# Row scatters in pairs behind the Fourier steps, and the first rows of the second part turned during the last batch

## The chip, the cores and the metric

The kernel runs on one core of a Trainium2 chip. The metric is the device time of one execution in microseconds. The kernel before takes 3161.35 us, the median of 3 runs (3157.11 to 3165.08).

## The reference

The three stages of the reference are chained; each takes the rows of the one before it. In short:

```python
# x: (8, 3072, 256)
X = np.fft.fft(np.fft.fft(x, axis=1), axis=2).real       # 24576 rows of 256
# mixture of experts: 8 experts, 256 -> 1024 -> 256, the best one only
do_compute = X @ w_skip > 0                               # other rows pass unchanged
e_idx = argmax(X @ w_gate);  gate = softmax(...)[e_idx]
out[do_compute] = X + gate * (relu(X @ w1[e]) @ w2[e])    # e = e_idx of the row
# feed-forward layer with a rational activation, 256 -> 2048 -> 256
h = out @ w_in
P = a0 + a1*h + a2*h**2 + a3*h**3
Q = 1 + |b0|*|h| + |b1|*h**2
return (P / (Q + 1e-6)) @ w_out
```

## The kernel before

All matrix products run on TensorE (PE) in f16 with each f32 operand split into a high and a low f16 half, three products for one. The program has two parts that follow each other.

*The Fourier stage* goes through the 8 batches. A batch is 12 steps of the loop over `n` (12 x 8 + 2 passes in all, since the third transform runs `LA` = 2 steps behind). In a step, `s1` makes a part of the first transform of the *next* batch (two of three steps do, and ACT and DVE or PE bring it to the tiles o1h and o1l), `s2` makes the second transform of two groups of 128 rows, and `s3` the third transform of the step two back. `s2` ends with an ACT conversion of the PSUM tile u to the f16 tile o2h (L264) and a DVE subtraction for the low half o2l; both live in a pool of three buffers. `s3` reads them on PE and writes finished rows of 258 floats (256 values, the row's number and its gate) into row buffers, of which some lie in the space of the weights `mw`, others in the tile `third`.

POOL does two things in this stage. From the second batch on it makes the low half xl of the input for three of eight chunks (`by_pool`, L202; the others are made on DVE). And it scatters the finished rows to their place in the array XS in DRAM: experts' rows sorted by expert from its beginning, rows that skip the experts from `SKIP0`. The scatters are indirect DMAs, issued by POOL, 24 in a batch with 128 rows each (L361). Their addresses come from `route_steps`, a generator that is started when a batch is finished and is advanced once per step: seven pieces of softmax, comparison and prefix sums, then one pair of scatters per advance. So the scatters of batch b are written at steps 12b+20 to 12b+31; those of batch 6 begin at step 92, and what is left of them behind the last step (97) is written out at one go (`for r in late`). The eighth batch is scattered in the second part, three at a time, between its steps.

Each engine works through its instructions in the order in which the code issues them, and a wait blocks everything behind it on its engine. Nothing reorders, so the code's order is the order on each engine. DMAs that the SP or ACT engine issues stand in that engine's row too: a DMA that waits for its input blocks the ones behind it.

*The second part* takes tiles of 512 rows (of XS) through the feed-forward layer, eight steps a tile, 384 in all, and the expert layer beside it. Its first tile is rows that skip the experts: `load_skip(0)` loads them after the scatters of batches 0 to 5, `z_begin` calls `split_turned`, which casts the rows to f16 on ACT (L885), subtracts on DVE (L886) and turns high and low halves with one transposing DMA from SP (L888). The first matmul of the part, `u<-turned,wi` (L897), needs the turned rows and wi, the high and low halves of the layer's first weights, which SP loads at L675 just ahead of wo (L676). Those weights were decoded from the input's bytes by `decode_steps` during the Fourier stage, through the tiles wf, wm and ws.

Two variables keep row positions: `carry` counts the rows that each expert and the skip group have so far, and for the skip rows the first positions are kept free of later batches by a maximum, so that a tile of rows may be loaded while later scatters still run (the groups `scat` and `scat7` say which DMAs need no order among each other).

Of the kernel before, what the change touches and what calls it, by code (L numbers as in the profile page):

```python
# [8 lines left out]
F32 = mybir.dt.float32  # L9
F16 = mybir.dt.float16  # L10
I32 = mybir.dt.int32
AF = mybir.ActivationFunctionType
ALU = mybir.AluOpType
# [9 lines left out]
NG = 24  # L23
TILE = 512
# [105 lines left out]
def program(tc, x, w_skip, w_gate, w1, w2, w_in, w_out, a, b, f1, cs, tw, tok, ut, small, lt8, slot, out):  # L130
# [3 lines left out]
    with es:  # L134
# [16 lines left out]
        scat = []  # L151

        fa = ExitStack()
        xp = fa.enter_context(tc.tile_pool(name="xp", bufs=4))
# [3 lines left out]
        o2p = fa.enter_context(tc.tile_pool(name="o2p", bufs=3))  # L158
        low = fa.enter_context(tc.tile_pool(name="low", bufs=1))
        low.tile([128, 4 * ROW], F32, name="below")  # L160
        rwp = fa.enter_context(tc.tile_pool(name="rwp", bufs=1))
# [85 lines left out]

        o2 = {}

        def s2(bb, gp):  # L250
            u = ps.tile([128, 2, 512], F32, tag="u", name="u")
            for s in range(2):
                g = 2 * gp + s
                o = u[:, s, 0:CB]
                n = 0
                for h in range(2):
                    lh = o1[bb, "h"][:, h].rearrange("p c q -> p (c q)")[:, g * 128:g * 128 + 128]
                    ll = o1[bb, "l"][:, h].rearrange("p c q -> p (c q)")[:, g * 128:g * 128 + 128]
                    for st, mv in ((lh, 0), (lh, 1), (ll, 0)):
                        pe.matmul(o, lhsT=st, rhs=f2t[:, h, mv, :], start=(n == 0), stop=(n == 5))  # L260
                        n += 1
            th = o2p.tile([128, 2, CB], F16, tag="o2h", name="o2h")
            tl = o2p.tile([128, 2, CB], F16, tag="o2l", name="o2l")
            act.activation(th[:], u[:, :, 0:CB], AF.Copy, scale=2.0 ** -8)  # L264
            dve.scalar_tensor_tensor(out=tl[:], in0=u[:, :, 0:CB], scalar=2.0 ** -8, in1=th[:], op0=ALU.mult, op1=ALU.subtract)
            o2[bb, gp] = (th, tl)

        rows = {}
# [50 lines left out]
        def route_steps(bb, new_u, per=2):  # L319
# [30 lines left out]
            dve.tensor_tensor(out=rk, in0=u[:, 0, 0:216].rearrange("p (g c) -> p g c", c=9), in1=carry[:, None, :].to_broadcast([128, NG, 9]), op=ALU.add)  # L350
            dve.tensor_tensor(out=carry[:], in0=carry[:], in1=u[:, 0, 216:225], op=ALU.add)
            if bb == B - 3:
                dve.tensor_scalar(out=carry[:, 8:9], in0=carry[:, 8:9], scalar1=float(SKIP0 + R0 * TILE), scalar2=None, op0=ALU.max)
                dve.tensor_scalar(out=carry[:, 0:1], in0=carry[:, 0:1], scalar1=float(R1 * HALF), scalar2=None, op0=ALU.max)
# [4 lines left out]
            yield  # L359
            for g in range(NG):  # L360
                i = pool.indirect_dma_start(out=XS[:, :], out_offset=IndirectOffsetOnAxis(ap=si[:, g:g + 1], axis=0),  # L361
                                            in_=rws[g // 4][:, g % 4, :], in_offset=None, bounds_check=NROWS - 1, oob_is_err=False)
                if scat:
                    tc.declare_no_dep(i.ins, group="scat", reason="every slot is given once")
                tc.add_to_no_dep_group("scat", i.ins)
                if bb >= B - 2:
                    tc.add_to_no_dep_group("scat7", i.ins)
                scat.append(i.ins)
                if g % per == per - 1:
                    yield  # L370

        def decode_steps():
# [13 lines left out]
            for n in range(8):  # L386
# [5 lines left out]
                f = wp.tile([128, 1024], F32, tag="wf", name="wf")  # L392
                m = wp.tile([128, 1024], F32, tag="wm", name="wm")
                fi = f[:].bitcast(I32)
                dve.tensor_scalar(out=fi, in0=hw, scalar1=3, scalar2=0x3FFFFFFF, op0=ALU.logical_shift_left, op1=ALU.bitwise_and)
                dve.scalar_tensor_tensor(out=fi, in0=hw, scalar=-0x40000000, in1=fi, op0=ALU.bitwise_and, op1=ALU.bitwise_or)
                yield
                act.activation(m[:], hw.bitcast(F32), AF.Abs)
                dve.scalar_tensor_tensor(out=fi, in0=lw, scalar=29, in1=fi, op0=ALU.logical_shift_right, op1=ALU.bitwise_or)
                yield  # L400
                dve.scalar_tensor_tensor(out=f[:], in0=m[:], scalar=TINY, in1=f[:], op0=ALU.is_ge, op1=ALU.mult)
                yield
                sc = 16.0 if n < 4 else 256.0
                st = wp.tile([128, 2, 1024], F16, tag="ws", bufs=2, name="ws")
                act.activation(st[:, 0, :], f[:], AF.Copy, scale=sc)
# [195 lines left out]
        s1_lo()  # L601
        late = []
        prep = decode_steps()
        coeff = coefficients()
# [4 lines left out]
        for n in range(12 * B + LA):  # L609
            bb, gp = divmod(n, 12)  # L610
            s1_hi()
            if bb < B:
                s2(bb, gp)
            if n >= LA:
# [23 lines left out]
            if n >= 12:  # L638
                next(coeff, None)
                if n % 4 == 0:  # L640
                    next(coeff, None)
        for r in late:
            for _ in r:
                pass
# [11 lines left out]
        wk = pool_of("wk", 1)  # L656
        xtp = pool_of("xtp", 2)
        xsp = pool_of("xsp", 2)
# [163 lines left out]

        xt = {}

        def load_skip(s):
            t = xtp.tile([128, 4, ROW], F32, tag="xt", name="xt")
            if s < R0:
                i = sp.dma_start(out=t[:], in_=XS[SKIP0 + s * TILE:SKIP0 + (s + 1) * TILE, :].rearrange("(p r) c -> p r c", p=128))
                tc.declare_no_dep(i.ins, group="scat7", reason="the last batches write behind these rows")
                if s == 0:  # L830
                    after(i.ins, scat[:NG * (B - 2)])
                tc.add_to_no_dep_group("early", i.ins)
            else:
                r = reg(sp, C_SKIP + s, NROWS - TILE)
                i = sp.dma_start(out=t[:], in_=rows_of(r, TILE))
                after(i.ins, fills)
            xt["S", s] = t
# [43 lines left out]

        def split_turned(src, nr, tag):

            rows = rsp.tile([128, 2, nr, D], F16, tag=tag, name="rows")
            act.activation(rows[:, 0], src, AF.Copy)  # L885
            dve.tensor_tensor(out=rows[:, 1], in0=src, in1=rows[:, 0], op=ALU.subtract)  # L886
            t = xsp.tile([128, 2, nr, 2, 128], F16, tag=tag, name="turned")
            sp.dma_start_transpose(out=t[:].rearrange("p l r h c -> p (l r h) c"), in_=rows[:].rearrange("p l r d -> p (l r d)"))  # L888
            return t[:, 0], t[:, 1]
# [29 lines left out]
        def moe_begin(t):  # L919
            return split_turned(t[:, :, 0:D], 2, "m")  # L920

# [44 lines left out]
        def z_begin(src, ids, n):  # L966
            Z[n] = dict(x=split_turned(src[:, :, 0:D], 4, "z"), ids=ids)

# [97 lines left out]

        for s in range(2):
            load_skip(s)
        last = route_steps(B - 1, lambda: psm.tile([128, 2, D], F32, tag="m", name="acc"), 3)
# [188 lines left out]
```

## Time and profile before

| | |
|---|---|
| median of 3 runs | 3161.35 us |
| the profiled execution | 3152.81 us |
| its span in the trace | 3151.0 us |
| PE busy | 2944.4 us (93%) |
| DVE busy | 2816.8 us (89%) |
| ACT busy | 2536.1 us (80%) |
| POOL busy | 1391.3 us (44%) |

The span is the time from the first to the last instruction that the trace holds; the profiled execution took 1.8 us more. PE, DVE and ACT are the matrix, vector and activation engines, POOL is GpSimd, and SP issues DMAs. The busy shares are averages over two parts with different limits: in the Fourier stage, up to about 520 us, every engine has idle time, and in the second part PE has little. The granted clock is TensorE's, as a share of 2.4 GHz: 1.00 is that level, 0.50 is 1.2 GHz.

### The profile page before, as it was taken

Reading aid. Unit: us, or ns where it says so; the run is one execution under the profiler, and the core shown is the slowest. Engines: PE = TensorE matmul, PEld = TensorE weight load, DVE = VectorE, ACT = ScalarE, POOL = GpSimd, SP = SyncE. Lnnn points to the kernel's source line nnn. Section 1 sums busy time; section 2 is a strip of 40 time slices with the busy share of each in tenths; the row PEclk is TensorE's granted clock in tenths of the full one; section 3 lists DMA queues with packets and bytes.
Section 4 is the critical chain, followed back from the end, with each engine's and each line's share of the span. In section 5 each row is a group of like instructions: output and inputs, shape, how many; then the busy total and the mean of one; then the engine's idle time right before and its main releaser. Section 6 shows DMA issues by size and latency. Waiting matters only on the chain.

```text
span 3151.0 us, 56948 instructions
## 1 busy us (share of the span) xinstructions
PE 2944.4 (93%) x22994; PEld 2146.2 (68%) x22994; DVE 2816.8 (89%) x2969; ACT 2536.1 (80%) x2758; POOL 1391.3 (44%) x796
## 2 busy tenths in 40 slices
PE   8877864899999999999999999999999999999995
PEld 7666642577667777777777777777777777777764
DVE  6767644999999999999999999999999999999896
ACT  7666634698879889889889888888888888888884
POOL 0455534544334444444444444444444444444444
PEclk9989877999999999999999999999999999999998
DMA  8444443322312222213222311112112111211100
GB/s 237 148 145 133 157 161 114 92 84 68 108 41 68 55 88 85 67 45 93 82 58 65 86 43 34 40 57 67 35 41 81 45 31 41 84 38 28 31 18 14
DMA packets 230368, 236.85 MB, mean 75 GB/s; under 512 B 166995, under 2 KB 190932, under 8 KB 227156
## 3 DMA queue, kind: packets, MB, share of 16 engines
q1 hardware_dynamic: 209364, 174.23, 20.3%
q0 software_dynamic: 18432, 50.55, 4.6%
q10 hardware_dynamic: 2304, 8.39, 0.7%
q8 instruction: 181, 2.97, 0.4%
q14 instruction: 87, 0.71, 0.1%
HBM read 190.69 MB, written 77.05 MB: 85 GB/s over the span
## 4 chain that ended last, share of the span: by engine, by line
PE 75%; DVE 13%; issue 5%; ACT 3%; DMA 3%; another core or an unknown queue 1%; POOL 0%; SPq 0%; DVEq 0%; ACTq 0%; POOLq 0%
PE accz L907 26%; PE u L897 26%; PE acc L907 7%; PE e L897 7%; DVE gh L1000 4%; PE u L260 3%; DVE T L982 2%; DVE V L1005 2%; DMA out<-ob,ids 2%; PE u L245 1%; DVE gl L1012 1%; PE u L310 1%; DVE hl L915 1%; PE u L308 1%
## 5 line engine op out<-in xcount | busy, mean ns | idle before, releaser
L1006 POOL TENSOR_TENSOR V<-T,V 128x1024 f32<-128x1024 f32 x384 | 913.5, 2379 | 1369.8 <-DVE V L1005 1364.8
L897 PE MATMUL u<-turned,wi 128*128 128x512 f16 x4608 | 1065.3, 381 | 38.6 <-DMA turned<-rows 20.3
L907 PE MATMUL accz<-wo,gh 128*128 128x256 f16 x6144 | 1032.4, 273 | 5.9 <-ACT ob L1028 5.9
L907 PE MATMUL accz<-wo,gl 128*128 128x256 f16 x3072 | 839.9, 273 | 20.4 <-DVE gl L1012 18.0
L1000 DVE SCALAR_TENSOR_TENSOR gh<-T,co,Y 128x1024 f16<-128x1024 f32 x384 | 804.5, 2095 | 0.0
L897 PEld LDWEIGHTS <-wi 128*128 128x128 f16 x4608 | 452.7, 98 | 508.9 <-issue 50.7
L980 ACT ACTIVATE T<-u,co 128x1024 f32<-128x1024 f32 x384 | 462.8, 1205 | 331.3 <-PE u L897 202.5
L907 PEld LDWEIGHTS <-gh 128*128 128x128 f16 x6144 | 603.1, 98 | 159.3 <-issue 8.5
L982 DVE SCALAR_TENSOR_TENSOR T<-T,co,u 128x1024 f32<-128x1024 f32 x384 | 487.6, 1270 | 68.0 <-ACT Y L981 61.4
L1012 DVE SCALAR_TENSOR_TENSOR gl<-V,co,Y 128x1024 f16<-128x1024 f32 x384 | 489.0, 1274 | 28.8 <-POOL V L1006 28.8
L1005 DVE SCALAR_TENSOR_TENSOR V<-V,co,gh 128x1024 f32<-128x1024 f32 x384 | 490.3, 1277 | 0.0
L986 ACT ACTIVATE V<-Y,co 128x1024 f32<-128x1024 f32 x384 | 440.4, 1147 | 25.8 <-DVE gl L1012 25.6
L990 ACT ACTIVATE Y<-V,co 128x1024 f32<-128x1024 f32 x384 | 441.2, 1149 | 0.0
L981 ACT ACTIVATE Y<-u,co 128x1024 f32<-128x1024 f32 x384 | 426.3, 1110 | 0.0
L994 ACT ACTIVATE Y<-Y 128x1024 f32<-128x1024 f32 x384 | 404.3, 1053 | 0.0
L907 PEld LDWEIGHTS <-gl 128*128 128x128 f16 x3072 | 301.4, 98 | 60.1 <-DVE gl L1012 22.1
L897 PE MATMUL e<-turned,mw 128*128 128x256 f16 x2496 | 307.7, 273 | 8.1 <-DMA turned<-rows 8.1
L907 PE MATMUL acc<-mw,hh 128*128 128x256 f16 x1664 | 278.1, 273 | 0.0
L897 PEld LDWEIGHTS <-mw 128*128 128x128 f16 x2496 | 244.8, 98 | 37.3 <-issue 8.4
L1029 POOL DMA_INDIRECT out<-ob,ids x192 | 232.8, 1213 | 64.1 <-issue 46.4
L907 PE MATMUL acc<-mw,hl 128*128 128x256 f16 x832 | 226.8, 273 | 0.0
L361 POOL DMA_INDIRECT xs<-mw,rt x132 | 136.2, 1032 | 115.0 <-DVE rt L358 43.5
(201 smaller groups left out, 2942.5 us busy)
## 6 DMA issues: line engine op xcount, KB each, us to landing
mw<-wd SPq DMA_DIRECT2D x50, 2048.0 KB
xt<-in_x SPq DMA_DIRECT2D x64, 384.0 KB
xm<-xs SPq DMA_DIRECT2D x52, 258.0 KB
wf<-in_moe_w SPq DMA_DIRECT2D x48, 256.0 KB
wd<-ws SPq DMA_DIRECT2D x48, 256.0 KB
xt<-xs SPq DMA_DIRECT2D x22, 516.0 KB
wd<-ws ACTq DMA_DIRECT2D x16, 512.0 KB
wr<-in_moe_w_in SPq DMA_DIRECT2D x4, 1024.0 KB
```

Of the source, the lines that this page charges most:

```text
L897: pe.matmul(u[:, s, :], lhsT=sta, rhs=mv[:, :, k, :], start=(n == 0), stop=(n == 5))
L907: pe.matmul(acc[:, r, :], lhsT=sta[:, c], rhs=mv, start=(first and r % 2 == 0 and s == 0 and n == 0), stop=(last and s == nf - 1 and n == ...
L980: act.activation(d["T"], d["u"], AF.Square, scale=A[0], bias=A[1])
L981: act.activation(d["Y"], d["u"], AF.Abs, scale=A[4])
L982: dve.scalar_tensor_tensor(out=d["T"], in0=d["T"], scalar=A[2], in1=d["u"], op0=ALU.add, op1=ALU.mult)
L986: act.activation(d["V"], d["Y"], AF.Square, bias=A[5])
L990: act.activation(d["Y"], d["V"], AF.Ln, bias=A[6])
L994: act.activation(d["Y"], d["Y"], AF.Exp, scale=-1.0)
L1000: dve.scalar_tensor_tensor(out=h[:], in0=d["T"], scalar=A[a0], in1=d["Y"], op0=ALU.add, op1=ALU.mult)
L1005: dve.scalar_tensor_tensor(out=d["V"], in0=d["V"], scalar=A[c], in1=h[:], op0=ALU.add, op1=ALU.mult)
L1006: pool.tensor_tensor(out=d["V"], in0=d["T"], in1=d["V"], op=ALU.subtract)
L1012: dve.scalar_tensor_tensor(out=l[:], in0=d["V"], scalar=A[a0], in1=d["Y"], op0=ALU.add, op1=ALU.mult)
```

## The change

The change has two halves.

*Pairs behind the steps.* In the batches 0 to 6, a POOL copy of one column (`tick`) stands ahead of every pair of scatters. It reads the o2h that the step before made (`seen[0]`), so the pair can't go before that step's conversion on ACT is done. The copy is a reader of o2h, and ACT's conversion three steps later, which writes the same buffer, waits for it.

*The first 512 rows.* At step 86 SP loads the first skip rows (`row0`) behind the scatters of batches 0 to 3; at step 92 ACT casts them, at step 93 DVE subtracts and SP turns them (`turned0`). The second part begins with these instead of casting and turning its own. So that these rows are final by then, `carry` for the skip group gets a lower limit after batch 3, and the group `scat7` takes the scatters from batch 4 on.

To make room, wm now lies in the tile ws, a spacer pool `low` is gone, and the second part's tiles xt and turned alternate between two pools with one buffer each, of which one (`xta`, `xza`) is made before the Fourier stage.

```diff
+        xta = es.enter_context(tc.tile_pool(name="xta", bufs=1))
+        xza = es.enter_context(tc.tile_pool(name="xza", bufs=1))
...
-        low = fa.enter_context(tc.tile_pool(name="low", bufs=1))
-        low.tile([128, 4 * ROW], F32, name="below")
...
+        seen = [None]
+        tick = cst.tile([128, 1], F32, name="tick")
...
+            return th
...
+            if bb == 3:
+                dve.tensor_scalar(out=carry[:, 8:9], in0=carry[:, 8:9], scalar1=float(SKIP0 + TILE), scalar2=None, op0=ALU.max)
...
             for g in range(NG):
+                if g % per == 0 and bb < B - 1:
+
+                    pool.tensor_copy(out=tick[:].bitcast(F16)[:, 0:1], in_=seen[0][:, 0, 0:1])
                 i = pool.indirect_dma_start(out=XS[:, :], out_offset=IndirectOffsetOnAxis(ap=si[:, g:g + 1], axis=0),
                                             in_=rws[g // 4][:, g % 4, :], in_offset=None, bounds_check=NROWS - 1, oob_is_err=False)
                 if scat:
                     tc.declare_no_dep(i.ins, group="scat", reason="every slot is given once")
                 tc.add_to_no_dep_group("scat", i.ins)
-                if bb >= B - 2:
+                if bb >= 4:
...
-                m = wp.tile([128, 1024], F32, tag="wm", name="wm")
+                st = wp.tile([128, 2, 1024], F16, tag="ws", bufs=2, name="ws")
+                m = st[:].rearrange("p l n -> p (l n)").bitcast(F32)
...
-                act.activation(m[:], hw.bitcast(F32), AF.Abs)
+                act.activation(m, hw.bitcast(F32), AF.Abs)
...
             s1_hi()
+            seen[0] = this
             if bb < B:
-                s2(bb, gp)
+                this = s2(bb, gp)
...
+            if n == 86:
+                row0 = xta.tile([128, 4, ROW], F32, tag="xt", name="xt")
+                i = sp.dma_start(out=row0[:], in_=XS[SKIP0:SKIP0 + TILE, :].rearrange("(p r) c -> p r c", p=128))
+                tc.declare_no_dep(i.ins, group="scat7", reason="the later batches write behind these rows")
+                for sc in scat[:4 * NG]:
+                    tc.add_manual_dep(i.ins, sc.name, SYNC, reason="the rows")
+                tc.add_to_no_dep_group("early", i.ins)
+            if n == 92:
+                f = wp.tile([128, 1024], F32, tag="wf", name="wf")
+                half = f[:].bitcast(F16).rearrange("p (l r d) -> p l r d", l=2, r=4)
+                act.activation(half[:, 0], row0[:, :, 0:D], AF.Copy)
+            if n == 93:
+                dve.tensor_tensor(out=half[:, 1], in0=row0[:, :, 0:D], in1=half[:, 0], op=ALU.subtract)
+                turned0 = xza.tile([128, 2, 4, 2, 128], F16, tag="z", name="turned")
+                sp.dma_start_transpose(out=turned0[:].rearrange("p l r h c -> p (l r h) c"), in_=half.rearrange("p l r d -> p (l r d)"))
...
-        xtp = pool_of("xtp", 2)
+        xtp = pool_of("xtp", 1)
+        xzb = pool_of("xzb", 1)
...
-        xt = {}
+        xt = {("S", 0): row0}
 
         def load_skip(s):
-            t = xtp.tile([128, 4, ROW], F32, tag="xt", name="xt")
+            t = (xta, xtp)[s % 2].tile([128, 4, ROW], F32, tag="xt", name="xt")
...
-                if s == 0:
+                if s == 1:
...
-            Z[n] = dict(x=split_turned(src[:, :, 0:D], 4, "z"), ids=ids)
+            x = split_turned(src[:, :, 0:D], 4, "z", (xza, xzb)[n % 2]) if n else (turned0[:, 0], turned0[:, 1])
+            Z[n] = dict(x=x, ids=ids)
...
-        for s in range(2):
-            load_skip(s)
+        load_skip(1)
```

What moves on the engines is shown at three places. On POOL, at the start of the program, the first xl and then the scatters of batch 0 (in a row "x10" stands for ten of the same kind that follow each other). Before:

```order
L202 TENSOR_TENSOR xl<-xt,xh 96x1024 x4
L361 DMA xs<-mw,rt 132096x258 x10
L202 TENSOR_TENSOR xl<-xt,xh 96x1024
L361 DMA xs<-mw,rt 132096x258 x2
L202 TENSOR_TENSOR xl<-xt,xh 96x1024
L361 DMA xs<-mw,rt 132096x258 x4
```

On POOL at the same place after the change:

```order
L203 TENSOR_TENSOR xl<-xt,xh 96x1024 x4
L369 COPY tick<-o2h 128x1
L370 DMA xs<-mw,rt 132096x258 x2
L369 COPY tick<-o2h 128x1
L370 DMA xs<-mw,rt 132096x258 x2
L369 COPY tick<-o2h 128x1
```

The ten scatters that stood without anything between them are now five pairs, each behind a copy; the xl stand where they stood.

On ACT, the last steps of the last batch, with the semaphores that each instruction waits for (DVE, PE, Pool and Activation are engines, DMAHW queues of DMAs); ev is the third transform's way out of PSUM. Before:

```order
L264 ACTIVATE o2h<-u 128x552 [waits DVE_49,PE_49]
L314 ACTIVATE ev<-u 128x276 [waits DVE_49,PE_49,Activation_49]
L264 ACTIVATE o2h<-u 128x552 [waits DVE_49,PE_49]
L314 ACTIVATE ev<-u 128x276 [waits DVE_49,PE_49,Activation_49] x3
L433 DMA wd<-ws 128x2048
L885 ACTIVATE rows<-xt 128x1024 [waits DMAHW4_49,DMAHW2_49]
```

On ACT in the last batch after the change:

```order
L267 ACTIVATE o2h<-u 128x552 [waits DVE_49,PE_49,Pool_49]
L318 ACTIVATE ev<-u 128x276 [waits DVE_49,PE_49,Activation_49]
L664 ACTIVATE wf<-xt 128x1024 [waits DMAHW7_49]
L267 ACTIVATE o2h<-u 128x552 [waits DVE_49,PE_49,Pool_49]
L318 ACTIVATE ev<-u 128x276 [waits DVE_49,PE_49,Activation_49]
```

The conversion to o2h waits for POOL as well, and the cast of the first rows (L885 before) stands four conversions ahead of the last one (L664).

On SP, the queue that loads the weights and the rows, from the last raw weights (wr) to the beginning of the second part. Before:

```order
L420 DMA wr<-in_moe_w 128x4x256 x2
L675 DMA wi<-wd 128x8192
L676 DMA wo<-wd 128x8192
L828 DMA xt<-xs 128x1032 x2
L888 DMA_TRANSPOSE turned<-rows 128x16x128
L828 DMA xt<-xs 128x1032
```

On SP at the same place after the change:

```order
L429 DMA wr<-in_moe_w 128x4x256 x2
L656 DMA xt<-xs 128x1032
L668 DMA_TRANSPOSE turned<-wf 128x16x128
L703 DMA wi<-wd 128x8192
L704 DMA wo<-wd 128x8192
L856 DMA xt<-xs 128x1032 x2
```

The load of the first rows and their turning stood behind the loads of wi and wo and now stand ahead of them.

## Rows read from the trace of the kernel before

**Rows 1.** The page: span, busy times, and PE's busy tenths in 40 slices.

```profile
span 3151.0 us, 56948 instructions
...
PE 2944.4 (93%) x22994; PEld 2146.2 (68%) x22994; DVE 2816.8 (89%) x2969; ACT 2536.1 (80%) x2758; POOL 1391.3 (44%) x796
...
PE   8877864899999999999999999999999999999995
```

**Rows 2.** Windows: stretch, length, PE PEld DVE ACT POOL busy, clock, DMA share, GB/s.

```profile
31.58:72.03 40.45, 38.73 (x476) 32.06 (x474) 29.82 (x54) 33.68 (x50) 2.14 (x1) 0.99 0.75 232
72.03:124.02 51.99, 44.54 (x524) 35.45 (x522) 41.64 (x107) 37.40 (x56) 18.12 (x13) 0.94 0.52 158
124.02:185.01 60.99, 47.70 (x526) 37.40 (x525) 39.50 (x102) 37.16 (x55) 32.27 (x28) 0.91 0.46 141
...
302.35:368.51 66.16, 50.18 (x525) 38.93 (x523) 43.85 (x103) 37.83 (x56) 32.05 (x27) 0.87 0.45 138
368.51:448.46 79.95, 51.42 (x524) 38.72 (x522) 33.65 (x94) 36.40 (x54) 45.20 (x41) 0.79 0.43 141
448.46:516.42 67.96, 31.34 (x325) 25.73 (x323) 31.39 (x96) 16.09 (x31) 23.41 (x24) 0.75 0.43 153
...
124.02:448.46 324.44, 242.71 (x2609) 188.71 (x2608) 200.45 (x502) 187.22 (x279) 174.83 (x150) 0.87 0.46 142
```

**Rows 3.** POOL timeline: start, length, instruction, and idle time before it in brackets.

```profile
149.67 0.97 POOL L361 DMA_INDIRECT xs<-third,rt  x1 [0.31 <-issue]
150.63 0.13 POOL L574 MEMSET co<- 128x1 f32 x1
150.95 0.97 POOL L361 DMA_INDIRECT xs<-third,rt  x1 [0.19 <-issue]
```

**Rows 4.** Windows inside POOL's runs of scatters.

```profile
408.10:413.20 5.10, 5.10 (x65) 4.26 (x63) 4.80 (x8) 2.87 (x6) 4.12 (x4) 1.00 0.22 78
433.70:438.90 5.20, 0.87 (x3) 0.41 (x4) 0.00 (x0) 0.00 (x0) 3.90 (x4) 0.50 0.28 102
...
129.90:140.30 10.40, 9.44 (x123) 8.04 (x122) 7.97 (x23) 8.51 (x13) 8.18 (x7) 1.00 0.55 156
...
480.42:505.72 25.30, 4.50 (x35) 2.60 (x32) 2.04 (x5) 1.03 (x2) 19.51 (x20) 0.62 0.29 104
413.20:438.90 25.70, 6.87 (x42) 3.74 (x41) 1.24 (x3) 2.08 (x3) 19.53 (x21) 0.60 0.42 144
```

**Rows 5.** Windows of four steps, edges at o2h conversions, with L361 (row scatters) alone.

```profile
102.32:124.02 21.70, 10.89 (x10) 0.86 0.52 170
189.09:204.42 15.33, 7.28 (x7) 1.00 0.35 105
372.26:389.55 17.29, 8.63 (x8) 1.00 0.69 222
```

**Rows 6.** Lines of POOL, 72 to 448 us: busy, mean ns, idle before.

```profile
L202 POOL TENSOR_TENSOR xl<-xt,xh 96x1024 f16<-96x1024 f32 x18 | 41.6, 2309 | 97.4 <-issue 55.3 <-ACT xh L194 42.0
```

**Rows 7.** Timelines of ACT, DVE and PE where the second part begins.

```profile
509.86 1.06 ACT L885 ACTIVATE rows<-xt 128x1024 f16<-128x1024 f32 x1
...
511.28 1.22 DVE L886 TENSOR_TENSOR rows<-xt,rows 128x1024 f16<-128x1024 f32 x1
...
516.42 1.86 PE L897 MATMUL u<-turned,wi 128*128 128x512 f16 x4 [20.34 <-DMA turned<-rows]
```

**Rows 8.** SP timeline: the load of wi and the turn of the first rows.

```profile
445.27 0.45 SPq L675 DMA_DIRECT2D wi<-wd  x1
...
512.52 1.74 SPq L888 DMA_TRANSPOSE turned<-rows  x1
```

**Rows 9.** Window in which the loads of wi and wo ran.

```profile
446.00:464.00 18.00, 12.21 (x126) 10.13 (x125) 10.13 (x27) 7.68 (x15) 0.00 (x0) 0.96 0.88 350
```

More of the change, by code (lines that the diff above doesn't have):

```diff
@@ L397, in decode_steps @@
                 yield
-                act.activation(m[:], hw.bitcast(F32), AF.Abs)
+                act.activation(m, hw.bitcast(F32), AF.Abs)
                 dve.scalar_tensor_tensor(out=fi, in0=lw, scalar=29, in1=fi, op0=ALU.logical_shift_right, op1=ALU.bitwise_or)
                 yield
-                dve.scalar_tensor_tensor(out=f[:], in0=m[:], scalar=TINY, in1=f[:], op0=ALU.is_ge, op1=ALU.mult)
+                dve.scalar_tensor_tensor(out=f[:], in0=m, scalar=TINY, in1=f[:], op0=ALU.is_ge, op1=ALU.mult)
                 yield
                 sc = 16.0 if n < 4 else 256.0
-                st = wp.tile([128, 2, 1024], F16, tag="ws", bufs=2, name="ws")
                 act.activation(st[:, 0, :], f[:], AF.Copy, scale=sc)
@@ L602, in program @@
         late = []
+        this = None
         prep = decode_steps()
@@ L880, in fill, with split_turned @@
                     yield
-        def split_turned(src, nr, tag):
+        def split_turned(src, nr, tag, to):
             rows = rsp.tile([128, 2, nr, D], F16, tag=tag, name="rows")
@@ L886, in split_turned @@
             dve.tensor_tensor(out=rows[:, 1], in0=src, in1=rows[:, 0], op=ALU.subtract)
-            t = xsp.tile([128, 2, nr, 2, 128], F16, tag=tag, name="turned")
+            t = to.tile([128, 2, nr, 2, 128], F16, tag=tag, name="turned")
             sp.dma_start_transpose(out=t[:].rearrange("p l r h c -> p (l r h) c"), in_=rows[:].rearrange("p l r d -> p (l r d)"))
@@ L919, in moe_begin @@
         def moe_begin(t):
-            return split_turned(t[:, :, 0:D], 2, "m")
+            return split_turned(t[:, :, 0:D], 2, "m", xsp)
         def moe_steps(t, w, xh, xl, xf, ids, k):
```

## The prediction

> **What bounds the kernel now.** I read the page first, then the windows view cut at the o2h conversions (L264) that open the batches, then the POOL timeline, then short windows inside POOL's runs of scatters. The span is 3151.0 us; the second part, where TensorE is 9 tenths or more busy nearly throughout, takes from about 520 us to the end [rows 1, 2]. No term of mine comes from there. Everything that the change touches lies before 540 us.
>
> In the Fourier stage no engine is full. The first batch, which runs before any row is scattered, takes 40.45 us for its 12 steps. The next takes 51.99 us and the five behind it 324.44, that is 64.9 each (the first 60.99, the last 79.95), although PE's count of matmuls hardly grows (476, then 524 to 526) and DVE is busy for 39.5 to 43.9 us in a batch of 61 to 66 [rows 2]. What grew is POOL: 24 row scatters per batch (L361), one every 1.28 us when they follow each other [rows 3].
>
> The short windows show where the time goes. With four scatters in a run, PE was busy in all 5.10 us. Some 20 scatters into the same run it was busy for 0.87 of 5.20 us, with DVE and ACT at nothing and the clock granted at 0.50, the 1.2 GHz level. From the fifth scatter to the 24th PE was busy for 6.87 of 25.70 us in this run and for 4.50 of 25.30 in the next batch's, DVE for one or two [rows 4]. The DMA engines are only 0.28 to 0.42 busy there, so it is not their share that is short. Six scatters with two xl subtractions (L202) between them, 10.4 us, left PE 9.44 us busy [rows 4]. So a scatter alone holds nothing; a run of them, from about the fifth on, holds everything until it ends. What inside the chip does that no row here tells; I use it as an observation.
>
> **The change part by part.** *Pairs behind a step.* Each pair of scatters now stands behind a POOL copy that reads the previous step's o2h, so POOL can't run through ten or 24 scatters at a stretch while TensorE is at one step. In batches 1 to 6 this makes two scatters in each step. What a step then costs I take from two stretches of before that look so already: four steps from one o2h conversion to the fifth, 15.33 us with 7 scatters and 17.29 us with 8 [rows 5], together 4.08 us a step. Twelve are 48.9; I take 49.
> Batches 2 to 6 took 324.4 us [rows 2]; five of 49 are 245: 79.4 saved. In batch 1 the scatters begin with its ninth step, at 102.32 us [rows 5]; from there to 124.02 are 21.7 us for four steps, which become 16.3: 5.4 saved.
> Bounds: a step can't be shorter than DVE's work, 39.5 to 43.9 us a batch [rows 2]; at 42 the two sums are 114.4 and 7.7. At 4.32 a step, the slower stretch, they are 65.3 and 4.4.
>
> *What the pacing costs.* 84 copies of one column. The nearest row is a POOL memset of one column, 0.13 us, and the scatter behind it began 0.31 us after the one before had ended, as without it [rows 3]. A pair is then 2 x 1.28 + 0.13 + 0.16 = 2.85 us, and with three xl of 2.31 us per batch [rows 6] POOL has 12 x 2.85 + 6.9 = 41 us of work in 49. The copy is hidden as long as that stays below the batch. New is a wait on ACT: three o2h buffers, so the o2h of step n+2 waits for the copy of step n. Behind it in ACT's queue stand ev, the o1 pair and xh, and PE's third transform waits for o2h. POOL has to be two steps late before this bites, about 8 us.
> The shared port could make the copy dear. The Trainium skill, "SBUF — State Buffer", Who interferes with whom, says that a DVE instruction with two SBUF inputs and a GpSimd instruction that reads SBUF exclude each other for a whole instruction. Such an instruction takes 1.22 us here [rows 7]; by that rule a pair would be up to 4.07 us, beside a step of 4.08, so the sum would not move but its slack would be gone. Xl, which reads SBUF, has a mean of 2.31 us, and nothing here shows it waiting that long inside; I keep 2.85.
>
> *Last batch.* It begins at 448.46 us, and the second part's first matmul came 67.96 us later, at 516.42 [rows 2, 7]. Its own steps were short, as no x is left to transform, so POOL's 2.85 us a pair now nearly sets them: I take 3.5 us (between 2.85 and 4.08), 42 us for twelve. Two more third transforms, and PE is free at about 46 after the batch's start. The first 512 rows are cast and turned in steps 92 and 93, so the 1.06 us cast, the 1.22 us subtraction and the 4 us until the turned rows landed go from the end of the chain [rows 7]. In their place the loads of wi and wo are late: SP sent them off at 445.27 us, and now the turn of step 93 stands before them in its queue [rows 8], so they leave at about 33 + 1.2 + 1.7 = 36 after the batch's start. At the 350 GB/s of the stretch in which they ran [rows 9], 4.2 MB need 12 us; wi goes first, so the first matmul starts at about 47.
> But POOL's pairs are late then: at the last o2h eight pairs, 16 scatters and 23 us, are still to go, now with nothing to pace them, and from the fifth on they hold the engines up to about 67 after the start. PE worked for 0.18 to 0.27 of such time [rows 4]; from the run's fifth scatter (about 49) to 67 that is some 4 us of progress, and the rest waits for the end. That is worth a start at 62 in place of 68: 6 saved. Bounds: nothing held, a start at 47, 21 saved; all held and the weights late, 5 lost.
>
> *The rest.* wm now lies in the ws tile: its Abs waits for a write issued some five steps before. One DVE instruction more on 9 columns costs less than the 1.22 us of one on 1024 [rows 7]. Two xt tiles and two turned tiles remain two each in the second part. I give these zero; their cover is the 5 to 9 us (49 less DVE's 39.5 to 43.9) that DVE has left in a batch.
>
> *Sum.* 79.4 + 5.4 + 6 = 91 us off the profiled execution's 3152.8: 3062. The median shown, 3161.35, is 8.5 above that execution, so a median of 3070.
>
> **Rivals.**
> (a) *The engines are held by the rate, not by the run.* Before, 24 scatters per 64.9 us are 0.37 per us. If the chip takes no more than 0.40, pacing spreads the hold evenly and a batch stays at 60: 324.4 - 300 = 24 saved, nothing in the last batch: 3137. For it: that the batches with full scatters lie near each other. Against it: 6 scatters in 10.4 us, 0.58 per us, with PE 91% busy [rows 4].
> (b) *The hold is the profiler's.* Then the timed runs never had it, and only some 6 us at the joint go: 3155, no change. The Trainium skill, "NOTIFIC — the notification-queue block", 7.1 Overflow, says that a notification path that fills can stall the engine that produces the records. By that rule the profiled execution would be the longer one. It took 3152.8 us, and the timed runs 3157 to 3165: the trace speaks against it.
> (c) *POOL becomes the bound, and the kernel slower.* With the new wait POOL, ACT and PE form a ring. A batch took 324.4 / 60 = 5.41 us a step; POOL's step is 2.56 + 0.6 (xl) + the copy. From a copy of 2.25 us with its wait, the change loses. At 3 us a step is 6.2, five batches 370: 46 lost, 3207. For it: the new wait is real, and POOL stands behind ACT's xh already (42.0 us of idle time [rows 6]). Against it: two steps of slack, and 0.13 us for the nearest row.
>
> **How the numbers follow.** Forecast 0.78, with an own range of 3018 (114.4 + 7.7 + 21 saved) to 3096 (65.3 + 4.4 - 5); (a) 0.11; (b) 0.05; (c) 0.06. The range that leaves out (b), (c) and the forecast's edges reaches to (a): 3020 to 3140. A run of this kernel can be told from no change by about 0.3%, 9.5 us. Faster: forecast and (a), 0.89; within: (b), 0.05; slower: (c), 0.06.
>
> **What would show it.** In the profile after: no run of more than four scatters before the last batch; batches 2 to 6 of 45 to 53 us each, with DVE over 80% busy and the clock near 1; no idle of ACT before o2h that ends with POOL. The copies at about 0.1 us each. wi issued right behind the first turn, and a first matmul of the second part near 430 us (516.4 - 84.8 - 2 to 21 earlier). Wrong would be: a batch of 58 us or more with evenly spaced pairs (rival a), ACT's o2h waiting for tick (rival c), or the trace shorter by 90 us and the times not (rival b). The second part itself, 3151.0 - 516.4 = 2634.6 us, should not move.

## The result and the profile after

The changed kernel takes 3080.21 us, the median of 4 runs (3075.67 to 3089.53), beside 3161.25 us for the kernel before (4 runs, 3157.11 to 3165.08). The ratio is 0.9753, with a 95% interval of 0.9734 to 0.9771: 81 us less. Its profiled execution took 3081.34 us, 71.5 less than that of before; the difference to the 81 is that the profiled execution of before, 3152.81, lies below all four of its timed runs.

The page of the changed kernel, with the span, the busy times and PE's busy tenths in 40 slices, answers to [rows 1]:

```profile
span 3079.6 us, 57105 instructions
...
PE 2931.4 (95%) x22994; PEld 2137.1 (69%) x22994; DVE 2813.3 (91%) x2970; ACT 2534.4 (82%) x2758; POOL 1423.9 (46%) x880
...
PE   8888868999899999999999999999999999999996
```

The windows cut at the o2h conversions that open the batches answer to [rows 2], with the same columns (stretch, length, busy time of PE, PEld, DVE, ACT and POOL, clock, DMA share, GB/s). The last but one is the joint, and the last is batches 2 to 6 together.

```profile
32.05:72.75 40.70, 38.86 (x476) 32.20 (x474) 29.82 (x54) 33.75 (x50) 2.13 (x1) 1.00 0.72 224
72.75:117.05 44.30, 41.67 (x526) 34.70 (x524) 38.89 (x105) 37.24 (x55) 18.83 (x15) 1.00 0.57 172
117.05:170.55 53.50, 42.65 (x525) 34.71 (x523) 44.36 (x106) 37.10 (x56) 40.89 (x44) 1.00 0.56 167
...
337.24:391.03 53.79, 46.95 (x541) 38.46 (x539) 33.59 (x92) 36.38 (x55) 35.39 (x39) 0.94 0.58 179
391.03:429.40 38.37, 28.15 (x295) 22.53 (x294) 25.84 (x76) 13.46 (x26) 25.00 (x33) 0.95 0.43 136
429.40:460.00 30.60, 17.22 (x80) 7.57 (x79) 11.53 (x42) 11.42 (x14) 18.47 (x26) 0.67 0.82 314
117.05:391.03 273.98, 227.33 (x2624) 182.16 (x2622) 202.47 (x507) 186.87 (x280) 188.03 (x200) 0.95 0.54 165
```

Batch 1 went from 51.99 to 44.30 us and batches 2 to 6 from 324.44 to 273.98, that is from 64.9 to 54.8 us each, with nearly the same number of instructions on PE, DVE and ACT. The second part's first matmul, in the timeline of PE, shows where the joint is now, and what it waited for:

```profile
435.13 1.46 PE L925 MATMUL u<-turned,wi 128*128 128x512 f16 x3 [2.85 <-DMA wi<-wd]
```

It comes 44.1 us after the last batch's begin at 391.03, in place of 67.96. Behind it the time is partly given back. From the T of the second part's seventeenth step on (640.3 us before, 568.9 now, both to the end) the two traces are equally long; these are windows of before and of after:

```profile
640.30:3151.00 2510.70, 2463.86 (x18163) 1779.27 (x18161) 2383.05 (x2024) 2153.43 (x2232) 1110.89 (x560) 0.99 0.21 57
```

```profile
568.90:3079.60 2510.70, 2464.68 (x18163) 1778.13 (x18160) 2379.88 (x2024) 2152.79 (x2232) 1110.69 (x559) 0.99 0.20 57
```

From the first matmul to that step it was 640.3 - 516.4 = 123.9 us and is 568.9 - 435.1 = 133.8. So the 71.4 us of the span are: 7.7 in batch 1, 50.5 in batches 2 to 6, 23.9 in the last batch, less 9.9 in the first sixteen steps of the second part, and less 0.7 before batch 1. The 9.9 lie where POOL issues the last 16 scatters of batch 6 in a row, from 431 to 452 us, with no step left to pace them.

On POOL the copies took 0.29 us each on average, about twice the memset of [rows 3]. Only 16 of the 84 had to wait for their o2h, 34.9 us in all. These are a row of POOL's lines, 100 to 455 us (busy, mean ns, idle before), and the row that counts the waits for o2h (us in total, times):

```profile
L369 POOL COPY tick<-o2h 128x1 f16<-128x1 f16 x84 | 24.1, 287 | 34.9 <-ACT o2h L267 34.9
```

```profile
  POOL tick L369: 34.9, 16
```

They held up no o2h conversion. The profile names a copy as the end of one idle stretch of ACT, 1.11 us before the conversion at 251.66. But there are three o2h buffers, so the copy that this conversion needs is the one that read the o2h of three steps before, and that had ended at 243.97. Paired off like this over the whole stage, the copy had ended at least 4.2 us before the conversion each time. These are the two rows, of ACT's and of POOL's timeline:

```profile
251.66 0.63 ACT L267 ACTIVATE o2h<-u 128x552 f16<-128x552 f32 x1 [1.11 <-POOL tick L369]
```

```profile
243.77 0.20 POOL L369 COPY tick<-o2h 128x1 f16<-128x1 f16 x1
```

### The profile page after: what moved, and what is told of

The parts are those of the page before. It is cut to its first block, busy times and chain, and to the rows that moved or that the text cites. A ratio compares the mean times of both kernels' runs of the same rounds, so it can differ in the third digit from the quotient of the medians.

```text
span 3079.6 us, 57105 instructions
## 1 busy us (share of the span) xinstructions
PE 2931.4 (95%) x22994; PEld 2137.1 (69%) x22994; DVE 2813.3 (91%) x2970; ACT 2534.4 (82%) x2758; POOL 1423.9 (46%) x880
## 4 chain that ended last, share of the span: by engine, by line
PE 75%; DVE 14%; issue 4%; ACT 3%; DMA 3%; POOL 1%; another core or an unknown queue 0%; SPq 0%; ACTq 0%; DVEq 0%; POOLq 0%
PE u L925 27%; PE accz L935 27%; PE acc L935 8%; PE e L925 8%; DVE gh L1029 4%; PE u L263 3%; DVE T L1011 2%; DVE V L1034 2%; DMA out<-ob,ids 2%; PE u L246 1%; DVE gl L1041 1%; ACT o1h L236 1%; DVE hl L943 1%; PE u L314 1%
## 5 line engine op out<-in xcount | busy, mean ns | idle before, releaser
L1011 DVE SCALAR_TENSOR_TENSOR T<-T,co,u 128x1024 f32<-128x1024 f32 x384 | 487.6, 1270 | 65.2 <-ACT Y L1010 55.8
L935 PEld LDWEIGHTS <-hh 128*128 128x128 f16 x1664 | 162.7, 98 | 19.0
```

The lines of the kernel that those rows point to most:

```text
L935: pe.matmul(acc[:, r, :], lhsT=sta[:, c], rhs=mv, start=(first and r % 2 == 0 and s == 0 and n == 0), stop=(last and s == nf - 1 and n == ...
L1011: dve.scalar_tensor_tensor(out=d["T"], in0=d["T"], scalar=A[2], in1=d["u"], op0=ALU.add, op1=ALU.mult)
```

## The experiments

Twelve runs in five sessions, each session on another chip, with the kernel before run beside them each time. The first thing that they showed overturned the plan for the rest: on none of these five chips (which one gave the result is not recorded) did the kernel before take 3161 us. Its medians there are 3046.43, 3047.54, 3049.39, 3047.75 and 3046.03. So every ratio below is against a kernel before that is some 114 us faster than the one of the result, and what the change won there was not there to be won.

**The change in parts.** The first of the two kernels has only the copies, the second only the early turn.

```diff
+                if g % per == 0 and bb < B - 1:
+                    pool.tensor_copy(out=tick[:].bitcast(F16)[:, 0:1], in_=seen[0][:, 0, 0:1])
```

> The kernel before with the copies ahead of the pairs and nothing else of the change. Theory (a run of back-to-back scatters holds the engines, and the copies' waits break the runs): batches 1 to 6 as in the changed kernel, 44.3 and 5 x 54.8 us, so 58 us less than before, and some 5 us less in the last batch, where the rows are still cast and turned at the end: 3098 us, between 3088 and 3106. Rival (most of the gain is the early turn): not under 3130 us.

Measured: 3049.41 us beside 3046.43, ratio 1.0009 (0.9998 to 1.0021). No change.

> The changed kernel without the copies. Theory: runs of 24 scatters are back, batches 2 to 6 take 62 to 67 us each again; the early turn alone is worth 0 to 14 us, because the run of batch 6 holds the engines at the joint whatever has been turned: 3147 to 3161 us. Rival (the early turn brings the first matmul of the second part forward by 24 us and keeps it): 3135 to 3140 us.

Measured: 3042.55 us beside 3046.43, ratio 0.9988 (0.9976 to 1.0000). Neither expectation could be met, since both set out from 3161. What counts is its trace: the scatters run unpaced again, as in the kernel before, and batches 2 to 6 take 250.94 us together, 50.2 each, and not 62 to 67. This is their window:

```profile
117.71:368.65 250.94, 216.75 (x2609) 178.28 (x2607) 209.48 (x509) 187.65 (x280) 162.88 (x138) 0.97 0.59 177
```

**The copy without its wait.** The copy reads a constant tile.

```diff
-                    pool.tensor_copy(out=tick[:].bitcast(F16)[:, 0:1], in_=seen[0][:, 0, 0:1])
+                    pool.tensor_copy(out=tick[:].bitcast(F16)[:, 0:1], in_=nid[:, 0:1])
```

> The changed kernel with the copy reading a constant tile, so the same POOL instructions stand between the pairs and wait for nothing. Theory (it is the wait for a Fourier step that paces): runs last as before, each pair 2.7 to 2.9 us, the engines held from about the fifth scatter on: 3145 to 3165 us, like the early turn alone. Rival (an instruction between two pairs is enough to end the hold): 3075 to 3090 us.

Measured: 3043.43 us beside 3046.43, ratio 0.9992 (0.9982 to 1.0002). It can't tell the two theories apart where no run is held.

**Both kernels again.** Unchanged, to see whether the difference of 114 us belongs to the kernel or to the place where it runs.

> The kernel before, unchanged, looked at a second time. In the runs of the last four kernels it took 3046 us, 115 us less than in the runs that were predicted, and the unpaced scatters of the early turn alone held no engine. Theory A (the hold belongs to the chip or its state on which the kernel runs, not to the kernel): the time is either 3040 to 3055 us, with batches 2 to 6 of 48 to 52 us and no hold in the 24 scatters of batch 6, or 3155 to 3167 us with the hold; nothing between. Rival (the kernel before differs from the others in some way that I don't see): 3155 to 3167 us while the changed kernel beside it takes 3080.

> The changed kernel, unchanged, beside the kernel before. Theory A: where the kernel before takes 3046 us, the change is worth nothing and takes 3038 to 3050 us (pairs alone measured 1.0009 of before, the early turn with copies that wait for nothing 0.9992); where it takes 3161, the change takes 3080 again. Rival (pairs and early turn together gain what neither gains alone): 2960 to 2975 us beside 3046.

Measured: 3046.43 us (a single run) for the kernel before, and 3044.75 us for the changed one beside 3047.54, ratio 0.9993 (0.9983 to 1.0002). The theory that the hold belongs to the chip or its state is borne out: the same program has no hold here. In its trace the windows are the batches 1, 2 to 6 and the last, then 18 us from the fifth scatter to the eighteenth of a run of eighteen (349.46 to 372.54):

```profile
71.07:115.31 44.24, 41.62 (x525) 34.65 (x523) 38.81 (x103) 37.27 (x56) 17.63 (x12) 1.00 0.60 169
115.31:362.57 247.26, 214.93 (x2609) 176.44 (x2607) 208.33 (x507) 187.94 (x280) 163.41 (x137) 0.97 0.59 179
362.57:410.70 48.13, 30.33 (x326) 26.09 (x324) 31.59 (x96) 16.31 (x31) 29.34 (x29) 0.85 0.69 244
...
354.58:372.54 17.96, 16.47 (x185) 13.45 (x183) 12.03 (x30) 9.48 (x17) 13.99 (x14) 1.00 0.96 345
```

PE is busy for 16.47 of 17.96 us deep inside a run, where it was busy for 6.87 of 25.70 and 4.50 of 25.30 in [rows 4]. The second part is as long as ever: 2510.3 us from its seventeenth step on, against 2510.7 in the kernel before of the result. But for some 2 us, the whole difference between the two executions lies in the stretch with the scatters: 7.8 us in batch 1, 77.2 in batches 2 to 6 and 19.9 in the last.

What the hold looks like from inside is in the first trace of the kernel before, in PE's timeline at the run of batch 6 (start, length, instruction, idle time before it):

```profile
481.64 0.22 PE L309 MATMUL u<-o2l,twt 128*128 128x138 f16 x1 [0.43 <-issue]
482.36 0.23 PE L310 MATMUL u<-o2h,twt 128*128 128x138 f16 x1 [0.49 <-issue]
482.43 0.23 PE L308 MATMUL u<-o2h,twt 128*128 128x138 f16 x1
482.49 0.22 PE L309 MATMUL u<-o2l,twt 128*128 128x138 f16 x1
483.77 0.22 PE L310 MATMUL u<-o2h,twt 128*128 128x138 f16 x1 [1.05 <-issue]
...
483.95 0.22 PE L310 MATMUL u<-o2h,twt 128*128 128x138 f16 x1
485.22 0.22 PE L308 MATMUL u<-o2h,twt 128*128 128x138 f16 x1 [1.04 <-issue]
485.27 0.22 PE L309 MATMUL u<-o2l,twt 128*128 128x138 f16 x1
486.65 0.28 PE L310 MATMUL u<-o2h,twt 128*128 128x138 f16 x1 [1.15 <-issue]
```

Matmuls of one chain, on data that is there, come in groups of one to four, and the groups begin about 1.4 us apart, close to one scatter's 1.28. "issue" says that PE waited for nothing that the profile shows. So what is late is nothing that the profile follows, neither a semaphore nor data; that it is the engine's own next instruction is a guess. PE's waits of this kind (all rows with "issue" added up) come to 54.7 us in batches 2 to 6 of this trace and to 10.2 in the changed kernel's. In the two traces of the repeated pair, from another chip, there are none. Why one session has them and five others do not, no run here tells.

**All xl on DVE.** This was meant to free POOL, so that it does not fall behind the copies.

```diff
-POOLC = (2, 3, 4)
+POOLC = ()
```

> The changed kernel with all low halves of the input made on DVE, none on POOL. Theory (the batches take 54.8 us instead of the 49 that were forecast because POOL falls behind its copies while it makes xl or waits for xh, then catches up with four or five scatters in a row, which hold the engines again): POOL has 6.9 us less a batch, no step has more than three scatters, a batch takes 49 to 52 us: 3050 to 3067 us. Rival (DVE's own work sets the batch): three more DVE instructions of 1.22 us a batch less some 3 us of stalls beside POOL: batches of 54 to 57 us, 3078 to 3095 us.

Measured: 3033.54 us beside 3046.43, ratio 0.9954 (0.9937 to 0.9971). Faster, but on a chip that has nothing to catch up, so it had another reason than the one expected. Two more kernels looked for it: the same without the copies, and the edit alone on the kernel before.

> The changed kernel with all low halves of the input on DVE and without the copies ahead of the pairs. Two chips so far ran the kernel before in 3046 to 3048 us and held nothing in runs of scatters; the xl on DVE gained 0.46% there with the copies. Theory (where nothing is held, the copies and their waits are only a cost, and the gain came from the DVE instructions that no longer stand still beside an xl on POOL): beside a kernel before at 3046 us this takes 3024 to 3034 us, batches 2 to 6 of 46 to 47 us. Rival (the copies are what kept the batches short once POOL had no xl): 3036 to 3046 us. On a chip that holds (the kernel before at 3161) the theory of the held runs expects 3125 to 3150 us, as nothing paces the scatters.

Measured: 3034.35 us beside 3049.39, ratio 0.9953 (0.9936 to 0.9969).

> The kernel before with nothing changed but that all low halves of the input are made on DVE. On a chip that holds nothing (the kernel before at 3046 to 3050): theory (the 0.46% of the two runs with xl on DVE has nothing to do with the change) expects 3031 to 3040 us, 0.995 to 0.997 of before. Rival (it needs the early turn or the copies): 3044 to 3052. On a chip that holds (before at 3161): the runs of scatters then have no xl between them, and the theory of the held runs expects 3155 to 3200 us.

Measured: 3034.62 us beside 3047.75, ratio 0.9956 (0.9939 to 0.9972). So it is worth the same with and without the change. That the gain is DVE's, as was expected, is shown only in part. On the kernel before, batches 2 to 6, DVE instructions that read SBUF twice are far longer than their size explains; these are two of them (lines with busy time and mean ns), and under them the same two with xl on DVE, in the kernel with the copies.

```profile
L574 DVE TENSOR_TENSOR co<-co,rt 128x1 f32<-128x1 f32 x12 | 7.6, 634 | 0.0
L325 DVE TENSOR_TENSOR rt<-rt 128x192 f32<-128x192 f32 x5 | 6.2, 1245 | 0.2
```

```profile
L583 DVE TENSOR_TENSOR co<-co,rt 128x1 f32<-128x1 f32 x12 | 1.8, 150 | 0.0
L329 DVE TENSOR_TENSOR rt<-rt 128x192 f32<-128x192 f32 x5 | 1.8, 358 | 0.2
```

But the edit takes something off ACT too: where POOL makes the xl, ACT first scales the input in an instruction of its own (L192), and that goes with it. Here are its row in the kernel before, and the window of batches 2 to 6 with the edit alone, which answers to 115.31:362.57 above:

```profile
L192 ACT ACTIVATE xt<-xt 96x1024 f32<-96x1024 f32 x15 | 15.7, 1045 | 0.0
```

```profile
116.58:348.85 232.27, 209.13 (x2609) 174.13 (x2607) 201.88 (x522) 173.51 (x264) 137.48 (x122) 0.99 0.63 190
```

The five batches are 15.0 us shorter. DVE is busy for 6.4 us less, although it has 15 xl more, and ACT for 14.4 us less. Which of the two the gain comes from, no run separates.

In the changed kernel's trace a single one is seen beside an xl, in the timelines of POOL and DVE:

```profile
283.18 2.88 POOL L203 TENSOR_TENSOR xl<-xt,xh 96x1024 f16<-96x1024 f32 x1 [3.29 <-ACT xh L195]
...
283.99 2.10 DVE L583 TENSOR_TENSOR co<-rt 128x1 f32<-128x1 f32 x1
```

A one-column instruction took 2.10 us and ended with the xl. The Trainium skill, "SBUF — State Buffer", Who interferes with whom, says that a DVE instruction with two SBUF inputs and a GpSimd instruction that reads SBUF exclude each other for a whole instruction; these rows agree, in the direction that the prediction did not look in: DVE stood still for POOL's xl.

**The rest of batch 6 behind the second part's steps.** The last 12 scatters that are still to be written after step 97 go out four at a time, without copies, and the expert layer begins five steps later (`M0`).

```diff
-        for r in late:
-            for _ in r:
-                pass
+        rest, = late
...
-        M0 = 0
+        M0 = 5
...
+            if left[0]:
+                for _ in range(2):
+                    if next(rest, 1) == 1:
+                        left[0] = 0
...
```

> The changed kernel with the last 12 scatters of batch 6 put behind the first three steps of the second part, four at a time, instead of at one go, and the expert layer begun 5 steps later. In the changed kernel's trace these ran in a row from about 431 to 452 us and TensorE, which could have begun the second part at 435, got 17.2 us of work done in 30.6. Theory on a chip that holds (before 3161): 3066 to 3075 us, 5 to 14 less than the changed kernel. On a chip that holds nothing (before 3046): within 5 us of the changed kernel's 3045. Rival (the expert layer's later begin and its weights' load behind the scatters cost a step or two at the end): 3 to 10 us slower than the changed kernel on either.

Measured: 3050.75 us beside 3049.39, ratio 1.0007 (0.9998 to 1.0017), 6 us over the changed kernel of another session, or 4 us when each is set against the kernel before beside it. Both expectations allow for that on such a chip. The traces lean to the rival: set against the repeated changed kernel, the second part takes 129.7 us in place of 125.8 up to its seventeenth step and 2514.4 in place of 2510.8 from there on. Whether it wins 5 to 14 us on a chip that holds is open.

**Groups of eight.** As many scatters per batch, but eight behind one copy every fourth step.

```diff
-                if g % per == 0 and bb < B - 1:
+                if g % 8 == 0 and bb < B - 1:
...
+                    if g % 8 == 7:
+                        for _ in range(4):
+                            yield
...
```

> The changed kernel with the scatters of batches 0 to 6 in groups of eight behind one copy every fourth step, instead of two behind one copy every step; as many per batch. On a chip that holds (before 3161, changed 3080): the theory of the held runs expects four scatters of each group to hold the engines, some 3 x 4 us a batch more than pairs, 3110 to 3140 us; the rival (a limit on the rate over a whole batch) 3075 to 3085 us, as the rate is the same. On a chip that holds nothing: 3040 to 3052 us, like every grouping so far.

Measured: 3040.98 us beside 3047.75, ratio 0.9981 (0.9972 to 0.9991); batches 2 to 6 take 243.29 us together. It would have told a run from a rate on a chip that holds; on this one it shows that pairs are, if anything, a little worse than eights.

**Both together, and once more the copy without its wait.**

> The changed kernel with the xl on DVE and the scatters in groups of eight, the two edits that came out ahead where nothing is held (0.9954 and 0.9981 of before). If they add up: 0.993 to 0.995 of before, 3026 to 3034 us beside 3048. Rival (both free POOL and the waits on it, so the second finds nothing left): 0.995 to 0.997, 3033 to 3039 us. On a chip that holds (before 3161): 3095 to 3140 us, for the last four of each group.

Measured: 3031.67 us beside 3046.03, ratio 0.9950 (0.9934 to 0.9967). This is the lowest time of the study. The ratio stands on the border between the two expectations, and its interval overlaps that of xl on DVE alone, so whether the second edit adds anything is open.

> The changed kernel with the copy reading a constant tile, once more, in case this chip holds. On a chip that holds (before 3161): by the theory that the wait for a step paces, 3145 to 3165 us; by the rival that any instruction between two pairs ends the hold, 3075 to 3090 us. On a chip that holds nothing: 0.998 to 1.000 of before again.

Measured: 3043.59 us beside 3046.03, ratio 0.9991 (0.9981 to 1.0002); not a chip that holds either.

## Why the prediction was right, and where it was not

*The size and the sign.* Forecast were 91 us off the profiled execution and a median of 3070 in 3020 to 3140; the profiled execution lost 71.5 and the median is 3080.21. What was won is won where the prediction looked for it, in the stretch with scatters, and the windows show it. That breaking the runs won it is argued from the two traces of the result and not shown by a run of its own: the copies and the early turn were never run apart on a chip that holds. What speaks for it is that the trace after holds as strongly as the one before behind a fourth scatter (below) and has fewer scatters there. The forecast was read from one session's trace and is right for a session that holds; that the result came from such a one was luck, as on the chip of the repeated pair the same two kernels can't be told apart (0.9993). That the hold is the profiler's (rival b) is refuted, as the timed medians fell by 81 us.

*Batches 2 to 6: the term that was mis-sized.* The term was 79.4 us, from 49 us a batch, and its lower bound was 65.3 (65.2 by its own figures). It measured 50.5, below that bound. The 49 itself was right for a batch that nothing holds: on the chips without the hold the five batches take 247.26 us, 49.5 each, with the kernel before, and 246.6 with the changed one. Wrong was that the copies put two scatters into each step and so end the hold. They left 273.98 - 247.3 = 26.7 us of the 324.4 - 247.3 = 77.1. Only 16 copies of 84 waited. A copy waits for a step that is done, so once POOL is late, behind an xl that waits for xh, its next copies wait for nothing, and the pairs stand as close together as before.

Between one wait or xl and the next, the changed kernel's POOL timeline has two runs of ten scatters, six of eight and three of six from batch 1 to batch 6, two more eights in the last batch, and the sixteen at the end. Of the 50.5 us, 26.2 were won in the window of batch 6 alone (79.95 to 53.79), the only one of the five with a run of 24 in it before. In the other four the xl had split the scatters into runs of 10, 2, 4 and 8 already, and these gained 24.3 together. One of the eights, from 303.38 us, in POOL's timeline:

```profile
300.07 3.02 POOL L203 TENSOR_TENSOR xl<-xt,xh 96x1024 f16<-96x1024 f32 x1 [3.15 <-ACT xh L195]
303.04 0.18 POOL L369 COPY tick<-o2h 128x1 f16<-128x1 f16 x1
303.38 1.01 POOL L370 DMA_INDIRECT xs<-mw,rt  x1
304.69 0.98 POOL L370 DMA_INDIRECT xs<-mw,rt  x1 [0.30 <-issue]
305.66 0.20 POOL L369 COPY tick<-o2h 128x1 f16<-128x1 f16 x1
306.02 0.98 POOL L370 DMA_INDIRECT xs<-mw,rt  x1 [0.16 <-issue]
```

and the windows of its first and its second four scatters:

```profile
303.43:308.60 5.17, 4.89 (x57) 4.04 (x56) 4.40 (x13) 3.24 (x5) 4.40 (x5) 1.00 0.51 156
308.60:314.80 6.20, 4.63 (x50) 3.38 (x48) 4.45 (x21) 1.97 (x3) 5.21 (x7) 0.86 0.86 285
```

PE is busy for 95% of the first and 75% of the second. In two of the sixes the first four scatters left it busy for 92 and 100%, and the stretch from the fifth on for 36 and 35%:

```profile
189.80:194.98 5.18, 4.75 (x59) 4.11 (x59) 4.97 (x17) 1.88 (x4) 4.41 (x6) 1.00 0.54 157
194.98:198.70 3.72, 1.34 (x18) 0.85 (x16) 0.86 (x12) 0.02 (x1) 1.99 (x3) 1.00 0.88 212
207.89:213.00 5.11, 5.11 (x63) 4.25 (x61) 5.00 (x10) 3.24 (x7) 4.34 (x5) 1.00 0.56 163
213.00:217.00 4.00, 1.40 (x15) 0.85 (x13) 2.33 (x6) 1.84 (x3) 2.69 (x4) 1.00 0.51 176
```

That is no weaker than in the kernel before, where the fifth to the eighth scatter of the two runs of 24 left PE busy for 30 and 41%:

```profile
413.20:418.40 5.20, 1.54 (x15) 0.97 (x14) 0.50 (x2) 0.82 (x2) 3.91 (x5) 0.97 0.85 278
480.40:485.50 5.10, 2.07 (x22) 1.20 (x19) 1.33 (x4) 0.40 (x1) 3.90 (x4) 1.00 0.29 104
```

The forecast "no run of more than four scatters" was therefore wrong. How much of the 27 us is its price is not shown: PE's waits for nothing named are 10.2 us, and against the same five batches of the changed kernel on the other chip (246.60 us, PE 213.52 us busy at a clock of 0.98) PE was also busy 13.8 us longer for the same products, at 0.95. That catching up is the cause rests on these rows; the run that was to test it met a chip that holds nothing.

The length of a run is not all that decides. The run of ten from 103.95 to 120.59 us, one scatter every 1.85 us, held hardly anything: PE waited 0.4 us for nothing named, and batch 1 took 44.30 us, as on a chip without the hold. The two sixes, one scatter every 1.33 and 1.43 us, were held:

```profile
103.95:111.28 7.33, 7.33 (x101) 6.26 (x100) 6.68 (x15) 5.63 (x10) 6.40 (x7) 1.00 0.87 300
111.28:121.57 10.29, 8.71 (x100) 6.92 (x98) 9.17 (x18) 8.58 (x12) 9.07 (x8) 1.00 0.53 155
```

A reading of the prediction was wrong here too. In the 10.4 us of [rows 4] with PE 9.44 us busy there is one xl between the six scatters, not two, so they are runs of two and four, and they say nothing on a longer run. Nor did DVE come over 80% busy in these batches: it was 202.47 us of 273.98, 74%.

*Batch 1.* 5.4 forecast, 7.7 measured: 44.30 us, and 44.24 on a chip that holds nothing.

*The last batch.* 6 us forecast, 14.0 measured (23.9 less 9.9). The first matmul came 44.1 us after the batch's begin; the prediction had 47 for it, and took 62 because the remaining scatters were expected to hold it. Wi was the last to arrive, as forecast. The scatters then ran from 431 to 452 us and slowed the first steps, but PE made far more of that time than in [rows 4]: 11.26 us in the 15.51 from the fifth of those scatters on, at a clock of 0.83.

```profile
436.16:451.67 15.51, 11.26 (x58) 4.93 (x57) 6.27 (x29) 3.72 (x4) 12.90 (x17) 0.83 0.85 316
```

An instruction of the second part has 512 columns, one of the third transform 138, so an engine that gets few instructions would lose less here. But it got more of them as well, 58 matmuls in these 15.51 us and 35 in the 25.30 of [rows 4]; what made the difference was not tested. That the sum of 91 came within 20 us of the 71.5 owes something to this: 28.9 us too much in batches 2 to 6 stand against 2.3 and 8.0 too little in the other two terms. On the chip of the repeated pair, which holds nothing, the first matmul comes 41.5 us after the last batch's begin in place of 48.1, and 2.2 of these 6.6 us are given back by the seventeenth step (125.8 us in place of 123.6).

*The costs.* The copy takes 0.29 us, not 0.13, and its wait never held ACT: rival (c) had the right ring and met its slack, 4.2 us at the least. The pairs did not become 4.07 us long (a pair above takes 2.62, from 303.04 to 305.66); what grew longer beside POOL were DVE's small instructions. The second part, which the prediction wanted to stay at 2634.6 us, took 3079.6 - 435.1 = 2644.5: the 9.9 us of its first sixteen steps. Behind them it did not move.

*What stays open.* Whether run or rate decides (rival a) is not settled. A limit of 0.40 scatters per us over a whole batch is ruled out in this form, as 24 in 54.8 us are 0.44. That the scatters must be close as well as many fits the run of ten, and all of it rests on windows inside the two traces of the result. Nor is it known what makes the engines hold, whether that chip always does so, and how many do: it was seen in one session of six.

## What to carry to other kernels

A stretch in which all engines stand still while nothing in the profile makes them wait may belong to the chip or its state and not to the program; run the same program on a second chip before a change is credited with removing it. A wait paces a queue only while the queue is on time: once it is late, the waits that were to space it are already fulfilled. And a small vector instruction that is many times longer than its size explains is worth a look at what the neighbour on its port is doing.

## What the runs showed of the hardware

The same program took 3161.25 us in one session and 3046.0 to 3049.4 in five others, on five chips, and the two profiles of it put the difference into the stretch with the indirect scatters, in whose runs TensorE was busy for 0.18 to 0.27 of the time in the one and for 0.92 in the other. In the session with the hold, six scatters 1.33 us apart were enough: TensorE was busy for 92% of the first four's time and for 36% from the fifth on; ten scatters 1.85 us apart were not. One subtraction of one column on VectorE took 2.10 us beside a GpSimd subtraction of 2.88 us; moving three of these subtractions per batch from GpSimd to VectorE, where each costs 1.22 us, and with them three ScalarE instructions of 1.05 us away, made the kernel 0.44% to 0.47% faster on three chips.
